# Last chunk's weights requested round by round, a higher filler threshold and a refitted order in a single-core transformer block

## The chip, the core and the metric

The kernel runs on one core of one Trainium2 chip. A core has five instruction queues: TensorE (PE, matrix products), ScalarE (ACT), VectorE (DVE), GpSimd (POOL) and SyncE (SP), which here does nothing but issue transfers. Each executes its queue in order and waits on semaphores that other engines and transfers raise. The metric is the device time of one execution in microseconds (us); lower is better. Before the change the median of three runs is 804.7 us (804.57, 804.7 and 805.7).

## The reference

The program computes one transformer block with adaptive layer norm, on 2048 tokens of width 640, 32 heads of width 20, and a gated MLP of width 1536, all in bfloat16:

```
mod = silu(c) @ w_mod                       # six vectors: sa, ca, ga, sb, cb, gb
h = layernorm(x) * (1 + ca) + sa
q, k, v = split(h @ wqkv)                   # 32 heads of 20
p = softmax(q @ k.T * 20 ** -0.5)           # full attention, 2048 x 2048 per head
x = x + ga * ((p @ v) @ wo)
h = layernorm(x) * (1 + cb) + sb
x = x + gb * (((h @ w_gate) * (h @ w_up)) @ w_down)
```

## The kernel before, in words

**Tiling.** The query tokens are cut into six chunks (`CHUNKS`): two of 512 and four of 256. For every chunk there are eight items, each of four heads; the very last item is split into two halves of 128 queries. An item's scores are made in units of 128 x 512 numbers. Most units go in pairs through ACT, which takes the exponential of a 128x1024 tile (line 1548); the others, in groups of four called quads, get their exponential on DVE by integer arithmetic (lines 1572, 1604, 1612 and 1609, the last also as pieces on POOL, line 1624). Both kinds are then multiplied with V on PE (line 2177). How many quads an item has is fixed by `QUADS`, so the number of ACT exponentials, 812, is fixed too.

**The suffix.** When a chunk's attention is done, its `suffix` follows, in the shadow of the next chunk's attention: the output projection, the second layer norm, the transposed `h2T`, twelve gate-and-up rounds (one per 128 columns of the MLP width, called `fc` 0 to 11), and the down projection. In this text "round k" is the gate-and-up round of the preceding (fifth) chunk for `fc` = k, and "pair k" its two weight tiles, one of `w_gate` and one of `w_up`, 160 KB each. Rounds of the fifth chunk run while the sixth and last chunk's attention runs. PE executes a round as small matmuls on `h2Tt,stg` in line 961, between scores (line 1511) and products with V (line 2177).

**The weight buffers.** Chunks 0 to 4 read gate and up weights through three `stg` buffers for each of the two kinds: pair k+3 may be loaded when round k has been executed. The last chunk's suffix has no attention to hide behind, so most of its weights (`fc` 0 to 9, ten pairs, twenty transfers) get buffers of their own, `stx`, which lie in memory that the attention no longer needs: `fc` 0 to 4 in dead query tiles, the others in the region that the fourth chunk's suffix leaves. Its `fc` 10 and 11 go through `stg`. All are issued by SP in line 1917. SP also issues, for every finished item, four or five small transfers that gather the attention output into `Ocp` (line 1732), a chunk's input `xck` (line 1791) and the output (line 2056).

**What sets the order.** Nothing is scheduled by hand. `build_kernel` makes a list of tasks with durations, dependencies and priorities, and `Sched.run` plays the program through at build time with those durations; the order in which tasks start there becomes each engine's instruction order, and the chip then follows that order, waiting on semaphores. The duration given to a weight load on SP is 400 ns (the default in `dma`), to an `Ocp` transfer 720 ns. Of ready tasks an engine takes the lowest priority number: `Ocp` has 1.05 or 2, chunk four's weights 20 and a bit, the last chunk's 21 and a bit. PE is driven by `pick_pe`: scores first when they can start, then a filler if the modelled activity of the last 3413 ns is under `FILL_HARD`, then projection and MLP rounds if it is under `FILL_MIN`, then products with V, then rounds, then a filler again. A filler (`do_fill`, line 2510) is four matmuls on the identity matrix whose result is not read. `HAM_MIN` is the activity of a 3413-ns window under which the model treats the PE clock as halved; `PE_SWITCH` and `PV_W` are the modelled cost of changing the kind of matmul and of one product with V. `STAGE` overrides the planning parameters while a given item is the oldest unfinished one.

Of the kernel before, what the change touches and what calls it, by code (L numbers as in the profile page):

```python
# [7 lines left out]
ALU = mybir.AluOpType  # L8
AX = mybir.AxisListType
BF16 = mybir.dt.bfloat16  # L10
# [21 lines left out]
STEAL_END = 66197.894  # L32
STEAL_GAP = 200
HAM_W = 3413.3
HAM_MIN = 2550.0
LKTOL = 300.0


# [92 lines left out]
class Sched:  # L131

    def __init__(self):
        self.tasks = []
        self.order = {k: [] for k in ("sp", "act", "pe", "dve", "pool")}
        self.all = []
        self.free_at = {k: T0 for k in self.order}
        self.pend = {k: [] for k in self.order}
        self.readyl = {k: [] for k in self.order}
        self.t = 0.0  # L140
        self.n = 0
        self.progress = 0
# [8 lines left out]
        self.ncold = 0  # L151
        self.nfill = 0
# [197 lines left out]
def emit_program(nc, sched, nsem_dma=56):  # L350
# [123 lines left out]
CHUNKS = ((0, 512), (512, 512), (1024, 256), (1280, 256), (1536, 256), (1792, 256))  # L474
# [6 lines left out]
PV_KEEP = 2  # L481
# [34 lines left out]
D_LATE = 16  # L516
D_RES = 20
PVMIN, PVMAX, PVCAP = 2, 7, 12
# [34 lines left out]
LATEQ_F = 0.35  # L553
QUAD_GAIN = 0.597233983857778
NTERM = 2

STAGE = {
    0: {"D_LATE": 16, "PVMIN": 2, "X_LATE": -179.96, "XDPRIO": 1.343, "LKTOL": 300.0, "FILL_MIN": 4190.746, "HOLD": 95, "TPRIO": 0.75, "PVTOL": 249, "EAGER": 9, "X_HALF": 0.0, "XBACK": 0, "D_RES": 74, "PVCAP": 12, "PVMAX": 14, "STEAL_GAP": 200, "PV_KEEP": 2},
    2: {"DL": 0.376},
    4: {"HOLD": 53.4},  # L560
    5: {"HOLD": 88.7, "STEAL_GAP": 176.5},
    7: {"DL": 0.501},
    9: {"LKTOL": 115.1},
    10: {"X_HALF": 5.8},
    11: {"DL": 0.443, "EAGER": 4, "FILL_MIN": 3731.3, "X_HALF": 38.6},
    12: {"DL": 0.459, "LKTOL": 438.4, "STEAL_GAP": 303.4, "EAGER": 10, "X_HALF": 21.8},
    13: {"DL": 0.417, "FILL_MIN": 4496.3, "STEAL_GAP": 266.2, "X_HALF": 20.9},
    15: {"LKTOL": 166.0, "PVMAX": 5, "EAGER": 10, "XBACK": 1},
    16: {"PVCAP": 10, "PVMAX": 3, "EAGER": 10, "FILL_MIN": 5086.4},
    17: {"X_HALF": -35.2},  # L570
    18: {"EAGER": 3, "X_LATE": -36.1, "HOLD": 42.4, "PVMIN": 1},
    19: {"DL": 0.471, "EAGER": 2, "X_HALF": 94.7},
    20: {"DL": 0.391},
    21: {"EAGER": 6, "FILL_MIN": 4510.3, "X_HALF": 24.2, "D_LATE": 5},
    22: {"PVMAX": 7, "X_HALF": 147.8, "EAGER": 9, "X_LATE": -21.9, "HOLD": 66.8},
    23: {"HOLD": 124.7, "X_HALF": 14.5},
    24: {"DL": 0.464},
    25: {"DL": 0.549, "PV_KEEP": 3, "X_LATE": 36.2},
    26: {"DL": 0.411, "X_LATE": 65.8, "PVMAX": 3, "EAGER": 8},
    27: {"DL": 0.473, "XBACK": 1, "HOLD": 186.0, "FILL_MIN": 3881.8, "X_LATE": -1.8},  # L580
    28: {"X_HALF": 33.6, "FILL_MIN": 4310.0, "XBACK": 0},
    29: {"PVMAX": 7, "X_LATE": -9.2},
    30: {"X_LATE": -109.9, "HOLD": 140.4, "XBACK": 1},
    31: {"X_LATE": 202.7, "D_RES": 21},
    32: {"PVCAP": 11, "X_HALF": -25.7, "X_LATE": 197.5},
    33: {"DL": 0.442},
    34: {"PVMIN": 5, "X_HALF": 27.8, "XBACK": 1},
    35: {"X_HALF": -31.6, "PVMAX": 14},
    36: {"DL": 0.524},
    37: {"X_LATE": -50.4},  # L590
    40: {"XBACK": 1, "HOLD": 36.3},
    41: {"X_LATE": 52.1, "X_HALF": -52.1},
    44: {"X_LATE": -66.5, "EAGER": 4, "D_RES": 10},
    47: {"FILL_MIN": 5302.0},
    48: {"PVCAP": 14, "FILL_MIN": 3192.3},
}
XHALF = 1
STG_G0, STG_G, XC_G = 12, -10, -20
X_LATE = -24.052
X_HALF = 0.0  # L600
# [10 lines left out]
def build_kernel(nc, A_x, A_wqkv, A_wo, B_x, B_w_gate, B_w_up, B_w_down, c, w_mod, out):  # L611
# [7 lines left out]
    NC = len(CHUNKS)  # L619
# [6 lines left out]
    sc = Sched()  # L626
# [87 lines left out]
    DSl = [at("DSS", [128, 4 * 512], I16, d_off + (NB0 + i) * 4096) for i in range(NSS)]  # L714
# [64 lines left out]
    if NALT:  # L779
# [6 lines left out]
        nsq, nsx = nsx, len(stx)  # L786
# [13 lines left out]
    sSS = Slots(list(range(NSS)), "SS")  # L800
# [533 lines left out]
    item_info = {}  # L1334
# [231 lines left out]
    for qi, (it, us) in enumerate(dquads):  # L1566
        st_ = d_state[qi]
        for x, u in enumerate(us):
            cell = {}

            def fp1(e, st_=st_, x=x, cell=cell):
                return e.tensor_scalar(DBl[st_["slot"]][:, x * 512:(x + 1) * 512], bank(cell["b"]), EBIAS, 0.0,  # L1572
                                       op0=ALU.add, op1=ALU.max)
            tp = Task("dve", ps_cost(512), fp1, [], prio=0.8, name=f"P1.{qi}.{x}")
            tp.on_start = lambda task, cell=cell: G.done(cell["b"], task)
            u.task = (tp, cell)
            sc.left += 1
            st_["p1"][x] = tp
    for qi, (it, us) in enumerate(dquads):
        st_ = d_state[qi]  # L1580
        st_["src"], st_["ss"] = {}, {}
# [34 lines left out]
        if X_POOL and qi % X_POOL == X_POOL - 1 and qi < len(dquads) - X_LAST and all(  # L1616
                dquads[z][0] == it for z in range(qi, min(len(dquads), qi + X_TAIL + 1))):
            st_["xby"] = None
            for x in range(X_PIECES):
                w = 2048 // X_PIECES  # L1620

                def fxp(e, x=x, w=w, st_=st_):
                    d = DSl[st_["ss"][0]][:, x * w:x * w + w].bitcast(BF16)
                    return e.tensor_tensor(d, DBl[st_["slot"]][:, x * w:x * w + w].bitcast(BF16), d, ALU.mult)  # L1624
                t = Task("pool", w * POOL_NS + 180.0, fxp, [tm, te], prio=2.0 + .1 * qi + .01 * x, name=f"XP.{qi}")
                t.lk = 2
                t.cond = lambda st_=st_: st_["xby"] != "dve"

                def on_p(task, x=x, st_=st_):
                    if x == 0:  # L1630
                        st_["xby"] = "pool"
                        st_["xd"].dead = True
                        sc.left -= 1
                    xjob[0] = X_PIECES - 1 - x
                    if x == X_PIECES - 1:
                        sB0.done(st_["slot"], task)
                        st_["src"][0] = [task]
                t.on_start = on_p
# [8 lines left out]
            def on_x(task, o0=o0, st_=st_):  # L1647
                o0(task)
                st_["xby"] = "dve"
# [109 lines left out]
    def suffix(ci):  # L1759
# [148 lines left out]
        for fc in range(FT):  # L1908
            use_x = tail and fc < nsx
            wbuf, dm = [], []  # L1910
            for w_, wv in enumerate((wgv, wuv)):
# [4 lines left out]
                def f(e, wv=wv, fc=fc, cell=cell):  # L1916
                    return e.dma_start(cell["t"], wv[:, :, fc * 128:(fc + 1) * 128])
# [115 lines left out]
        for tl in range(ntl):  # L2033
# [5 lines left out]
            for (c_, w) in cuts:  # L2039
# [10 lines left out]
                if tail and TAILX:  # L2050
# [535 lines left out]
```

## Time and profile before

| What | Value |
|---|---|
| Median of the runs | 804.7 us |
| The profiled execution's own time | 806.1 us |
| Span from its first to its last instruction | 804.3 us |
| Mean granted PE clock | 0.998 |
| PE / ACT / DVE / POOL busy in the span | 786.4 / 762.8 / 688.5 / 361.9 us |
| ACT exponentials of line 1548 | 812, 746.8 us busy |
| Filler matmuls of line 2510 | 108, 9.7 us busy |
| Weight loads into `stx` | 20 of 160 KB, issued from 684.1 to 690.9 and from 715.4 to 730.0 us |

Positions in the program are given as microseconds from the start of the span. A row of the timeline has the start, the length, the engine, the line, the operation with its tiles, how many instructions were merged, and in brackets the idle time of the engine just ahead of it with what the profile holds to have ended it. "Busy" counts overlapping instructions once; PE is nearly always busy by this count because matmuls are pipelined and their ends are modelled, so a full PE row does not mean a PE at its peak.

### The profile page before, as it was taken

Reading aid. Unit: us, or ns where it says so; the run is one execution under the profiler, and the core shown is the slowest. Engines: PE = TensorE matmul, PEld = TensorE weight load, DVE = VectorE, ACT = ScalarE, POOL = GpSimd, SP = SyncE. Lnnn points to the kernel's source line nnn. Section 1 sums busy time; section 2 is a strip of 40 time slices with the busy share of each in tenths; the row PEclk is TensorE's granted clock in tenths of the full one; section 3 lists DMA queues with packets and bytes.
Section 4 is the critical chain, followed back from the end, with each engine's and each line's share of the span. In section 5 each row is a group of like instructions: output and inputs, shape, how many; then the busy total and the mean of one; then the engine's idle time right before and its main releaser. Section 6 shows DMA issues by size and latency. Waiting matters only on the chain.

```text
span 804.3 us, 34189 instructions
## 1 busy us (share of the span) xinstructions
PE 786.4 (98%) x14875; PEld 345.9 (43%) x14875; DVE 688.5 (86%) x1355; ACT 762.8 (95%) x847; POOL 361.9 (45%) x373
## 2 busy tenths in 40 slices
PE   8999999999999999999999999999999999998998
PEld 4433423332233232323444444455555554544567
DVE  7989797898999899999877888988898989796654
ACT  6899899999999999999999999999999999998951
POOL 2443436545464643234664433654653434635400
PEclk9999999999999999999999999999999999999999
DMA  9843212202341522101301232100342054527400
GB/s 297 241 122 79 66 53 67 63 24 70 106 107 45 152 66 52 42 7 47 72 18 23 47 78 55 39 16 24 97 88 56 24 121 90 109 58 159 89 22 18
DMA packets 136387, 60.49 MB, mean 75 GB/s; under 512 B 100703, under 2 KB 136239, under 8 KB 136239
## 3 DMA queue, kind: packets, MB, share of 16 engines
q1 hardware_dynamic: 135311, 57.16, 28.0%
q8 instruction: 118, 1.93, 1.0%
q10 hardware_dynamic: 928, 1.15, 0.4%
q14 instruction: 30, 0.25, 0.1%
HBM read 46.70 MB, written 8.99 MB: 69 GB/s over the span
## 4 chain that ended last, share of the span: by engine, by line
PE 60%; ACT 24%; DVE 9%; issue 4%; DMA 2%; SPq 1%; ACTq 0%; DVEq 0%
ACT PP L1548 24%; PE ps_all L1511 20%; PE ps_all L961 18%; PE ps_all L2177 14%; DVE DB L1572 3%; PE ps_all L957 3%; PE ps_all L1221 2%; DMA wm<-in_w_mod_dram 1%; DVE DSS L1612 1%; DVE DSS L1604 1%; DVE DSS L1609 1%; SPq L1732 1%; PE ps_all L2510 1%; PE ps_all L1118 1%; PE ps_all L1157 1%
## 5 line engine op out<-in xcount | busy, mean ns | idle before, releaser
L1548 ACT ACTIVATE PP<-ps_all 128x1024 bf16<-128x1024 f32 x812 | 746.8, 1145 | 7.5 <-PE ps_all L1511 5.2
L1624 POOL TENSOR_TENSOR DSS<-DB,DSS 128x512 bf16<-128x512 bf16 x264 | 300.1, 1157 | 335.3 <-DVE DSS L1612 276.6
L1572 DVE TENSOR_SCALAR DB<-ps_all 128x512 int16<-128x512 f32 x424 | 283.6, 683 | 60.7 <-PE ps_all L1511 58.3
L1511 PE MATMUL ps_all<-QT,KT 32*128 32x256 bf16 (+2 forms) x3136 | 319.1, 307 | 7.0 <-ACT PP L1548 4.1
L1511 PEld LDWEIGHTS ps_all<-QT,KT 32*128 32x128 bf16 x3136 | 89.2, 92 | 229.2 <-ACT PP L1548 191.5
L2177 PE MATMUL ps_all<-PP,Vf 128*32 128x256 bf16 (+2 forms) x2504 | 164.0, 311 | 0.6 <-DVE Vf L1310 0.6
L961 PE MATMUL ps_all<-h2T,stg 128*32 128x256 bf16 (+2 forms) x2272 | 122.3, 303 | 0.8 <-DMA stg<-in_B_w_up_dram 0.5
L2177 PEld LDWEIGHTS ps_all<-PP,Vf 128*32 128x32 bf16 (+1 forms) x2504 | 50.2, 94 | 81.7 <-issue 74.7
L2177 PE MATMUL ps_all<-DSS,Vf 128*32 128x256 bf16 (+1 forms) x1264 | 84.9, 313 | 0.0
L1604 DVE TENSOR_SCALAR DSS<-DB 128x2048 int16<-128x2048 int16 x106 | 73.6, 695 | 0.6
L1612 DVE TENSOR_SCALAR DSS<-DB 128x2048 int16<-128x2048 int16 x106 | 73.1, 690 | 0.0
L961 PEld LDWEIGHTS ps_all<-h2T,stg 128*32 128x32 bf16 x2272 | 51.4, 96 | 30.2 <-issue 20.3
L961 PE MATMUL ps_all<-wd,hprod 128*32 128x320 bf16 (+1 forms) x1384 | 63.2, 279 | 0.0
L1711 POOL TENSOR_TENSOR OTn<-OT,invT 128x256 bf16<-128x256 f32 (+1 forms) x42 | 34.8, 829 | 34.2 <-DVE invT L1709 34.2
L1609 DVE TENSOR_TENSOR DSS<-DB,DSS 128x2048 bf16<-128x2048 bf16 x40 | 49.3, 1231 | 0.0
L2177 PEld LDWEIGHTS ps_all<-DSS,Vf 128*32 128x32 bf16 (+1 forms) x1264 | 31.3, 96 | 20.1 <-issue 8.5
L961 PEld LDWEIGHTS ps_all<-wd,hprod 128*32 128x32 bf16 x1384 | 31.0, 96 | 18.0 <-issue 12.2
L961 PE MATMUL ps_all<-wV,hT 128*32 128x160 bf16 x1280 | 37.6, 234 | 0.6 <-DVE DB L1572 0.2
L1221 PE MATMUL ps_all<-hT,wk 128*32 128x512 bf16 (+1 forms) x360 | 31.6, 382 | 0.4 <-DVE DB L1572 0.2
L1221 PE MATMUL ps_all<-hT,wq 128*32 128x512 bf16 x375 | 31.4, 382 | 0.0
L961 PEld LDWEIGHTS ps_all<-wV,hT 128*32 128x32 bf16 x1280 | 24.0, 96 | 15.4 <-issue 8.4
L961 PE MATMUL ps_all<-wo,Ocp 128*32 128x320 bf16 (+1 forms) x628 | 30.1, 287 | 0.0
(131 smaller groups left out, 525.5 us busy)
## 6 DMA issues: line engine op xcount, KB each, us to landing
stg<-in_B_w_gate_dram SPq DMA_DIRECT2D x62, 160.0 KB
stg<-in_B_w_up_dram SPq DMA_DIRECT2D x62, 160.0 KB
KT<-k_rows SPq DMA_DIRECT2D x112, 32.0 KB
wm<-in_w_mod_dram SPq DMA_DIRECT2D x3, 800.0 KB
x<-in_A_x_dram SPq DMA_DIRECT2D x7, 320.0 KB
k_rows<-KPA SPq DMA_DIRECT2D x16, 128.0 KB
QT<-q_rows SPq DMA_DIRECT2D x32, 64.0 KB
wd<-in_B_w_down_dram SPq DMA_DIRECT2D x1, 1920.0 KB
```

Of the source, the lines that this page charges most:

```text
L957: return lambda e, b: e.matmul(ps[:, b, c0:c0 + n], lhs(), rhs(), start=st, stop=sp)
L961: return lambda e, b: e.matmul(ps[32 * x:32 * x + 32, b, c0 + o:c0 + o + w], lhs()[:, 32 * x:32 * x + 32], rhs() if w == n else rhs()[:, o ...
L1221: f = [lambda e, b_, k=k, x=x: e.matmul(ps[x:x + min(32, w - x), b_, :], wx[:, k, r0 + x:r0 + min(x + 32, w)], hT[tc][:, k, :], tile_posit ...
L1511: ems.append(lambda e, i=i, kt=kt: e.matmul(dstf()[:, i * u.n:(i + 1) * u.n], KT[32 * u.s:32 * u.s + 32, u.j, kt * 128:(kt + 1) * 128], QT ...
L1548: return e.activation(PPs[g % 2][:, cellp["p"], 0:nu * 512], ps[:, b0:b0 + nu, :].rearrange("p b c -> p (b c)"), AFT.Exp, scale=ESCALE)
L1572: return e.tensor_scalar(DBl[st_["slot"]][:, x * 512:(x + 1) * 512], bank(cell["b"]), EBIAS, 0.0, op0=ALU.add, op1=ALU.max)
L1604: return e.tensor_scalar(DSl[st_["ss"][0]][:, :], DBl[st_["slot"]][:, :], 0x7F, 0x3F00, op0=ALU.bitwise_and, op1=ALU.bitwise_or)
L1609: return e.tensor_tensor(d, DBl[st_["slot"]][:, :].bitcast(BF16), d, ALU.mult)
L1612: return e.tensor_scalar(DSl[st_["ss"][1]][:, :], DBl[st_["slot"]][:, :], 0x7F80, 2, op0=ALU.bitwise_and, op1=ALU.bitwise_or)
L1624: return e.tensor_tensor(d, DBl[st_["slot"]][:, x * w:x * w + w].bitcast(BF16), d, ALU.mult)
L1711: f3 = lambda e: e.tensor_tensor(OTn[:, 0:n].rearrange("p (b c r) -> p b r c", c=32, r=2), OT[:, 0:n].rearrange("p (b r c) -> p b r c", c= ...
L2177: ems.append(lambda e, i=i, kt=kt, stt=stt, stp=stp: e.matmul(ps[32 * s:32 * s + mc, bk, 0:u.n], Vf[:, (kt * H + 4 * u.j + s) * VW:(kt * H ...
```

## The change

Three things are changed, and a function is added.

1. The twenty `stx` loads no longer wait for the gathered attention output of the fifth chunk (`oc_ready`). The pair of `fc` waits instead for round `fc // 2` of the fifth chunk: pairs 0 and 1 for round 0, pairs 2 and 3 for round 1, and so on to pairs 8 and 9 for round 4. What frees the memory is waited for as before.
2. Fillers: `FILL_HARD` goes from 3000 to 3500, so a filler goes ahead of other PE work at a higher activity than before, and `HAM_MIN` from 2550 to 3000.
3. The order: `PE_SWITCH` goes from 102 to 105 ns, `PV_W` from 219 to 221 ns, and most entries of `STAGE` are replaced, those of the `DL` kind excepted.

The new function `maybe_sum` would add a quad's two DVE terms on POOL. It returns at once when an item has fewer than `SUM_LEFT` = 100 pieces left; an item has at most 64, so it never acts.

```
-PE_SWITCH = 102.0
+PE_SWITCH = 105.0
-PV_W = 219.0
+PV_W = 221.0
-HAM_MIN = 2550.0
+HAM_MIN = 3000.0
-FILL_HARD = 3000.0
+FILL_HARD = 3500.0
+SUM_LEFT, SUM_Q = 100, 0
 STAGE = {
-    0: {"D_LATE": 16, ..., "D_RES": 74, "PVCAP": 12, "PVMAX": 14, ...},
-    2: {"DL": 0.376},
-    4: {"HOLD": 53.4},
+    0: {"LKTOL": 300.0, ..., "PVCAP": 7, ..., "PVMAX": 14},
+    1: {"FILL_MIN": 2536.8, "XBACK": 2},
+    2: {"DL": 0.376, "FILL_MIN": 5326.4, "D_RES": 24, "PVMIN": 2, "STEAL_GAP": 118.3, "PVCAP": 9},
...
-    40: {"XBACK": 1, "HOLD": 36.3},
-    41: {"X_LATE": 52.1, "X_HALF": -52.1},
-    44: {"X_LATE": -66.5, "EAGER": 4, "D_RES": 10},
-    47: {"FILL_MIN": 5302.0},
-    48: {"PVCAP": 14, "FILL_MIN": 3192.3},
+    39: {"EAGER": 6, "X_LATE": -72.2, "XBACK": 3},
+    42: {"X_LATE": 34.4},
+    43: {"D_RES": 14, "X_HALF": -60.7, "LKTOL": 352.8},
+    45: {"PV_KEEP": 2, "X_HALF": -48.6, "LKTOL": 347.6},
 }
...
+    def maybe_sum(st_, qi, it, tx, te):
+        info = item_info[it]
+        if (qi, 1) not in info["dq"] or info["left"] < SUM_LEFT or sumq[0] + xjob[0] > SUM_Q:
+            return
...
                 t = dma("sp", int(STG_B * 128 * KD * 128 * 2), f,
-                        (sfx_done["qdead"] if fc < nsq else first) + oc_ready[(NC - 2, CHUNKS[-2][1] // 128 - 1)] if use_x else
+                        (sfx_done["qdead"] if fc < nsq else first) + sfx_done["ulist"][fc // 2:fc // 2 + 1] if use_x else
                         kp_use if ci == 0 else [], prio=16 + ci + .01 * fc,
...
         sfx_done["ul"] = u_last[-1:]
+        sfx_done["ulist"] = u_last
...
+                if jj and SUM_LEFT < 99 and st_["src"].get(0) is None:
+                    continue
```

More of the change, by code (lines that the diff above doesn't have):

```diff
@@ L151, in __init__ @@
         self.ncold = 0
+        self.nsum = 0
         self.nfill = 0
@@ L566 @@
[L566 to L574, printed above, removed]
@@ L584 @@
-    31: {"X_LATE": 202.7, "D_RES": 21},
-    32: {"PVCAP": 11, "X_HALF": -25.7, "X_LATE": 197.5},
+    0: {"LKTOL": 300.0, "PVMIN": 2, "X_HALF": 0.0, "D_RES": 74, "D_LATE": 16, "PVTOL": 249, "XBACK": 0, "STEAL_GAP": 200, "PVCAP": 7, "X_LATE": -179.96, "FILL_MIN": 4190.746, "EAGER": 9, "HOLD": 95, "PV_KEEP": 2, "XDPRIO": 1.343, "TPRIO": 0.75, "PVMAX": 14},
+    1: {"FILL_MIN": 2536.8, "XBACK": 2},
+    2: {"DL": 0.376, "FILL_MIN": 5326.4, "D_RES": 24, "PVMIN": 2, "STEAL_GAP": 118.3, "PVCAP": 9},
@@ new lines @@
+    3: {"HOLD": 89.7, "X_HALF": 95.8, "XBACK": 4},
+    6: {"PVMAX": 2, "PV_KEEP": 2, "FILL_MIN": 4261.9, "HOLD": 126.7, "D_LATE": 14},
+    7: {"DL": 0.501, "HOLD": 104.5, "PVMAX": 9, "PVTOL": 291.1},
+    9: {"PVCAP": 11, "X_LATE": -43.4},
+    10: {"STEAL_GAP": 236.0, "X_LATE": 27.2, "D_LATE": 16, "PVCAP": 19, "EAGER": 8, "FILL_MIN": 4539.8},
+    11: {"DL": 0.443, "PVTOL": 349.4, "X_LATE": 38.4},
+    12: {"DL": 0.459, "PVMIN": 1, "EAGER": 9},
+    13: {"DL": 0.417, "HOLD": 117.9},
+    15: {"PVMAX": 8, "EAGER": 8, "X_HALF": -45.4, "X_LATE": 143.1},
@@ new lines @@
+    19: {"DL": 0.471, "HOLD": 55.3, "X_LATE": -24.5},
+    20: {"DL": 0.391, "X_LATE": -10.9},
+    21: {"X_LATE": 161.4, "LKTOL": 262.0},
+    23: {"X_LATE": 127.5, "EAGER": 10, "HOLD": 62.1},
+    24: {"DL": 0.464, "EAGER": 6, "X_HALF": 82.8, "FILL_MIN": 4409.2},
+    25: {"DL": 0.549, "FILL_MIN": 3796.3, "X_LATE": 4.6, "EAGER": 10, "STEAL_GAP": 332.7, "D_RES": 9},
+    26: {"DL": 0.411, "HOLD": 92.2, "EAGER": 8, "PVMIN": 5, "XBACK": 0, "PVTOL": 374.0},
+    27: {"DL": 0.473},
+    29: {"HOLD": 88.3, "XBACK": 1, "PV_KEEP": 2, "X_HALF": 47.9, "EAGER": 6},
@@ L586 @@
+    30: {"FILL_MIN": 5256.4},
+    31: {"LKTOL": 323.3, "HOLD": 121.8, "XBACK": 1},
+    32: {"X_HALF": -47.6, "PVMIN": 7},
     33: {"DL": 0.442},
-    34: {"PVMIN": 5, "X_HALF": 27.8, "XBACK": 1},
-    35: {"X_HALF": -31.6, "PVMAX": 14},
+    35: {"X_LATE": -46.0},
     36: {"DL": 0.524},
-    37: {"X_LATE": -50.4},
-    40: {"XBACK": 1, "HOLD": 36.3},
-    41: {"X_LATE": 52.1, "X_HALF": -52.1},
-    44: {"X_LATE": -66.5, "EAGER": 4, "D_RES": 10},
-    47: {"FILL_MIN": 5302.0},
-    48: {"PVCAP": 14, "FILL_MIN": 3192.3},
+    38: {"X_LATE": 122.3},
@@ L1578, in build_kernel, with fsum, on_s @@
             st_["p1"][x] = tp
+    sumq = [0]
+    def maybe_sum(st_, qi, it, tx, te):
+        info = item_info[it]
+        if (qi, 1) not in info["dq"] or info["left"] < SUM_LEFT or sumq[0] + xjob[0] > SUM_Q:
+            return
+        info["dq"].remove((qi, 1))
+        info["left"] -= 1
+        for u in st_["units"]:
+            left_pv[(it, u.s)] -= len(u.kts)
+        sc.nsum += 1
+        sc.left -= 1
+        sumq[0] += X_PIECES
+        ts = []
+        for x in range(X_PIECES):
+            w = 2048 // X_PIECES
+            def fsum(e, x=x, w=w):
+                d = DSl[st_["ss"][0]][:, x * w:x * w + w].bitcast(BF16)
+                return e.tensor_tensor(d, d, DSl[st_["ss"][1]][:, x * w:x * w + w].bitcast(BF16), ALU.add)
+            t = Task("pool", w * POOL_NS + 180.0, fsum, [tx, te], prio=2.05 + .1 * qi + .01 * x, name=f"SP.{qi}")
+            t.lk = 2
+            def on_s(task, x=x):
+                sumq[0] -= 1
+                if x == X_PIECES - 1:
+                    sSS.done(st_["ss"][1], task)
+            t.on_start = on_s
+            ts.append(sc.add(t))
+        st_["src"][0] = ts
     for qi, (it, us) in enumerate(dquads):
@@ L1627, in build_kernel, with on_p @@
                 t.cond = lambda st_=st_: st_["xby"] != "dve"
-                def on_p(task, x=x, st_=st_):
+                def on_p(task, x=x, st_=st_, qi=qi, it=it, te=te):
                     if x == 0:
@@ L1637, in on_p @@
                         st_["src"][0] = [task]
+                        maybe_sum(st_, qi, it, task, te)
                 t.on_start = on_p
@@ L1645, in build_kernel, with on_x @@
             t.cond = lambda c0=c0, st_=st_: st_["xby"] is None and c0() and xjob[0] >= XBACK
-            def on_x(task, o0=o0, st_=st_):
+            def on_x(task, o0=o0, st_=st_, qi=qi, it=it, te=te):
                 o0(task)
+                maybe_sum(st_, qi, it, task, te)
                 st_["xby"] = "dve"
```

15 lines of the change are left out of this document (removed).

## The prediction

> **What bounds the kernel now.** I read the page first, its head and the rows by slices.
>
> ```profile
> span 804.3 us, 34189 instructions
> PE 786.4 (98%) x14875; PEld 345.9 (43%) x14875; DVE 688.5 (86%) x1355; ACT 762.8 (95%) x847; POOL 361.9 (45%) x373
> ...
> ACT  6899899999999999999999999999999999998951
> ```
>
> ACT is full from the second slice to the third-last, but for two: the fifth (80 to 100 us) and the 37th (724 to 744 us). ACT's exponentials are fixed in number, so they are the metre: the windows of 100 us hold 109 to 111 of them (x column) from 100 to 700 us, 0.91 to 0.92 us each. Here the change can win only where ACT stands idle. ACT's timeline shows where:
>
> ```profile
> 699.60 30.57 ACT L1548 ACTIVATE PP<-ps_all 128x1024 bf16<-128x1024 f32 x33
> 732.25 1.02 ACT L1548 ACTIVATE PP<-ps_all 128x1024 bf16<-128x1024 f32 x1 [2.07 <-PE ps_all L1511]
> 733.72 1.02 ACT L1548 ACTIVATE PP<-ps_all 128x1024 bf16<-128x1024 f32 x1 [0.45 <-PE ps_all L1511]
> 735.26 1.02 ACT L1548 ACTIVATE PP<-ps_all 128x1024 bf16<-128x1024 f32 x1 [0.51 <-PE ps_all L1511]
> 736.48 3.77 ACT L1548 ACTIVATE PP<-ps_all 128x1024 bf16<-128x1024 f32 x4 [0.20 <-PE ps_all L1511]
> ```
>
> The brackets add up to 3.23 us. By starts it is more: the last exponential before the hole began at 729.09 (its 1.09 us end at 730.17), the one at 736.48 is the fourth after it, so 7.39 us passed where four at 0.92 take 3.68: 3.7 us lost. PE's timeline has the cause:
>
> ```profile
> 728.99 0.29 PE L961 MATMUL ps_all<-h2Tt,stg 128*32 128x256 bf16 x4
> 731.42 0.46 PE L961 MATMUL ps_all<-h2Tt,stg 128*32 128x256 bf16 x12 [2.14 <-DVE DSS L1612]
> ```
>
> The windows of 2 us show what it costs (columns: stretch, length, busy of PE, PEld, DVE, ACT and POOL, granted clock, DMA share, GB/s):
>
> ```profile
> 730.00:732.00 2.00, 0.58 (x16) 0.37 (x16) 1.35 (x3) 0.17 (x1) 0.57 (x1) 1.00 0.86 196
> 732.00:734.00 2.00, 2.00 (x42) 1.18 (x42) 0.23 (x1) 1.30 (x2) 2.00 (x3) 0.59 1.14 228
> 734.00:736.00 2.00, 2.00 (x40) 0.91 (x28) 0.79 (x2) 1.49 (x2) 1.93 (x2) 0.56 0.06 14
> ```
>
> PE stands 2.14 us in front of round 4 (with 40 matmuls a round, half-width ones counted as halves, rounds 0 to 3 end at 718.6, 722.2, 726.6 and 729.3). The bracket names DVE, but PE's own semaphore wait there is on two transfers, pair 4, whose landing events are at 730.82 and 731.33. Behind that hole the clock is granted at 0.59 and 0.56 for two rows, which spreads the three later ACT gaps. Of the 3.7 us the wait is 3.16 - 0.92 = 2.2 (ACT starts at 729.09 and 732.25), the low clock the other 1.5. Why pair 4 is late stands in SP's timeline:
>
> ```profile
> 718.64 3.00 SPq L1732 DMA_DIRECT2D Ocp<-OcT  x4
> 721.69 1.38 SPq L1917 DMA_DIRECT2D stg<-in_B_w_gate_dram  x1
> ...
> 725.38 0.53 SPq L1917 DMA_DIRECT2D stx<-in_B_w_gate_dram  x1
> 725.95 0.53 SPq L1917 DMA_DIRECT2D stg<-in_B_w_gate_dram  x1
> 726.53 0.56 SPq L1917 DMA_DIRECT2D stg<-in_B_w_up_dram  x1
> ...
> 731.72 3.80 SPq L1732 DMA_DIRECT2D Ocp<-OcT  x5
> 735.57 0.48 SPq L1917 DMA_DIRECT2D stg<-in_B_w_gate_dram  x1
> ```
>
> Its buffer was free at 722.2, but it was issued at 725.95, behind pair 3 and four of the ten `stx` loads that SP was given at 715; then it took 4.8 us to land with those ahead of it. SP does not rest from 714.98 to 737: it is the short resource here, not the data rate alone.
>
> **The change, part by part.** *The requests.* Removed: ten `stx` loads at 684.1 to 691.5, when nothing waited behind them (the next issue, an `Ocp` at 692.50, was in time), so their leaving gains nothing; and the ten at 715 to 730. Added: four `stx` loads behind each of rounds 0 to 4, twenty in all, in the same 20 us in which SP must issue pairs 3 to 7 and nine `Ocp`. So the same stretch gets ten loads more, but no longer ahead of pairs 3 and 4.
>
> The queue by hand, with durations of this trace: an `Ocp` is 0.76 us (3.00 for four), and pairs go before `stx` by priority. A weight load costs SP from 0.57 us start to start (smooth rows) to 0.77 (13 of them from 721.69 to 731.72, the long issues of 1.38 and 2.03 us included). Three bursts of four, at 642.60, 654.07 and 664.08, took 0.55, 0.62 and 0.74; a batch after a round is such a burst, so I take 0.64. `OcT` is ready at 716.9, so four `Ocp` go to 720.05. Pair 3 and four `stx` end at 723.9; pair 4 is then issued to 725.2 instead of 727.1 and lands, 2.9 us after its second issue as in an empty queue (678.03 to 680.91), at 727.4. Round 4 can start at 729.3: the first hole closes. Its 2.2 and 1.5 us come back: -3.7.
>
> Next in line is pair 6. Five `Ocp` become ready at 728.0 and by priority go ahead of it. Ahead of it stand pairs 3, 4 and 5 (6 loads), ten `stx` and the nine `Ocp`: 720.05 + 16 x 0.64 + 3.85 = 734.1, its second issue at 734.8, landing 737.7. Without the hole, round 6 (started at 739.96 before) is due 3.7 us earlier, at 736.2. So PE waits 1.5 us there. Ends: 0.57 gives 736.6, a wait of 0.4, and none if the new order puts the `Ocp` behind it; 0.77 gives 740.1, 3.9 us. A wait of 1.5 is shorter than the 2.14 that cost the clock, so I count no low clock: +1.6 with the 0.1 by which ACT's loss exceeded PE's. Behind the waiting PE stand scores, so ACT pays all of it. Pair 7 then goes out ahead of the remaining `stx`, whose readers start at 781 us and wait for nothing.
>
> *Fillers.* The page has 108 matmuls of line 2510, 27 fillers; 17 of them lie in 400 to 500 us, where the window holds 109 exponentials against 110 or 111 elsewhere. One exponential, 0.9 us, over 17 fillers is 0.05 each at most. As many again as all 27 would cost 0 (ACT covers them) to 1.4 us (none covered); near the lower end, since the idle rows of ACT there total 0.2 us: +0.3. A gain is excluded where the clock stands at 1.00, which is everywhere but at the hole.
>
> *The order.* Two planned costs move by 1 to 3%, and `STAGE` is mostly new. No instruction is added or removed by this. Its cover is ACT's fullness: from 100 to 729 us the idle rows of ACT sum to under 1 us. What it can move is the spacing, 0.91 to 0.92, against 0.904 for back-to-back exponentials (685 x 0.014 = 9.6 us at stake), and the head, where PE sets the pace and ACT idles 2.1 us in 80 to 100 us. If each 100 us moves by half of the scatter seen between windows (half an exponential), six of them make 2.7 us either way, singly 0.45; as independent moves 1.1. I take 0, bounds -1.5 and +2.
>
> `maybe_sum` and the `HAM_MIN` constant add no instruction: 0.
>
> Sum: -3.7 + 1.6 + 0.3 + 0 = -1.8. The profiled execution took 806.1 us (span 804.3 and 1.8 around it) and lies 1.4 above the median, 0.17%; taken from it the sum gives 804.3, from the median 804.7 it gives 802.9. Less than 0.2%, 1.6 us, I call no change: the runs shown spread by 0.14%.
>
> **The rivals.** *All on time.* SP issues at 0.57 or the order lets pair 6 through: -3.7 + 0.3 = -3.4, 801.3. For it: the smooth rows; against: long issues came in every long stretch.
>
> *The wait moves and takes the clock along* (the other side). With 0.77 us a load round 6 waits 3.9 us, the clock falls again: 3.9 + 0.1 + 1.5 + 0.3 - 3.7 = +2.1, 806.8. It decides from a wait of 2.1, the one known to cost the clock: 2.1 + 0.1 + 1.5 + 0.3 - 3.7 = +0.3; slower by 0.2% it is from 3.4. For it: pair 6 was issued at 735.57 already, with the old order, and landed at 738.98; the old hole hid that. Against: this needs the worst stretch throughout.
>
> The Trainium skill, TensorE: Matmul & The Clock Gate, section "HAM oscillation", warns only of PE gaps over about 3.4 us, a whole idle window. By that rule a wait between 2.1 and 3.4 us would cost no clock, and the change would come to 804.8 at a wait of 3.4 us where the rows give 806.3. The trace speaks against it: 2.14 us were enough.
>
> *The first hole stays*, because another load precedes pair 4 in the new order: about 804.9 with fillers. Against: the tally has 1.9 us to spare at round 4.
>
> *The refitted order costs more than the requests bring*: +2 on top of the forecast, with uncovered fillers +1.1: 806.0. For it: planned durations (400 ns a load) are below every row; against: ACT's fullness.
>
> **How the numbers follow.** Forecast 0.40 (own range 801.7 to 804.1), all on time 0.20, wait with low clock 0.20, hole stays 0.08, order costs 0.12. Faster by over 1.6 us: 0.6 of the first, nearly all of the second, and 0.04 from a lucky order in the others: 0.48. Slower: 0.6 of the third, most of the last, little of the rest: 0.27. The remaining 0.25 is no change. The range runs from 800.6 (all on time with a little from the order) to 806.7 (nearly the clock case in full).
>
> **What would show it.** Right: all `stx` issues after 718, in fours; no PE gap at round 4; a PE gap of about 1.5 us at round 6 with pair 6 issued near 734; clock 1.00 throughout; 109 to 111 exponentials per 100 us. Wrong: a PE gap over 2 us near 736 with granted rows near 0.6; or windows of 100 us with 108 or 112; or a head in which the first hundred us hold more or fewer than 82 exponentials by over two.

## The result: slower by 0.8%, and the profile after

The changed kernel takes 810.9 us (median of 4 runs, 809.3 to 811.6) against 804.6 us before in the same session: a ratio of 1.0076, interval 1.0054 to 1.0098. It is 8.0 us above the forecast of 802.9 and outside its range. The profiled execution took 811.6 us, with a span of 809.8; before it was 806.1 and 804.3. The spans differ by 5.5 us, and that is what has to be found.

Line numbers have moved by a few: exponentials are now line 1544, scores 1507, products with V 2209, the rounds 957, weight loads 1946, `Ocp` transfers 1761, fillers 2542. The head of the page after and two of its rows of 40 slices:

```profile
span 809.8 us, 33954 instructions
PE 789.5 (97%) x14755; PEld 342.5 (42%) x14755; DVE 689.3 (85%) x1352; ACT 764.1 (94%) x848; POOL 370.8 (46%) x381
...
ACT  7899899999999999999999999999999999997951
PEclk9999999999999999999999999999999999999899
```

ACT's low digit still stands in slice 37 (729 to 749 us now), a 7 where it was an 8, and the row of the clock has an 8 in the slice behind it, where it was 9 throughout. The 812 exponentials are the same ones in both kernels, so the start of the n-th can be compared directly, and this gives a running account of what is won and lost (read from the starts of all exponentials in the two traces):

| n-th exponential | start before, us | after, minus before |
|---|---|---|
| 1 | 16.9 | -0.85 |
| 701 | 667.9 | +0.47 |
| 755 | 718.1 | -0.17 |
| 773 | 738.3 | -3.53 |
| 781 | 745.6 | -2.18 |
| 791 | 754.8 | +4.58 |
| 812 | 774.8 | +3.76 |
| end of the span | 804.3 | +5.5 |

Up to the 755th the two stay within 1.5 us of each other. Then the old hole is gone (-3.4), a little is lost at round 6 (+1.4), 6.8 us are lost in the next ten exponentials, 0.8 comes back, and a further 1.7 us is lost behind the attention. ACT's timeline of after shows the same place:

```profile
734.77 5.91 ACT L1544 ACTIVATE PP<-ps_all 128x1024 bf16<-128x1024 f32 x6
741.59 2.85 ACT L1544 ACTIVATE PP<-ps_all 128x1024 bf16<-128x1024 f32 x3 [0.90 <-PE ps_all L1507]
749.27 1.02 ACT L1544 ACTIVATE PP<-ps_all 128x1024 bf16<-128x1024 f32 x1 [4.83 <-PE ps_all L1507]
750.79 1.02 ACT L1544 ACTIVATE PP<-ps_all 128x1024 bf16<-128x1024 f32 x1 [0.50 <-PE ps_all L1507]
752.52 1.02 ACT L1544 ACTIVATE PP<-ps_all 128x1024 bf16<-128x1024 f32 x1 [0.71 <-PE ps_all L1507]
753.94 25.77 ACT L1544 ACTIVATE PP<-ps_all 128x1024 bf16<-128x1024 f32 x28 [0.40 <-PE ps_all L1507]
```

An idle 0.90 at round 6, then 4.83, and three exponentials that come 1.4 to 1.7 us apart instead of 0.92. PE's timeline names the two transfers:

```profile
739.42 0.41 PE L2209 MATMUL ps_all<-PP,Vf 128*32 128x256 bf16 x8
740.71 0.51 PE L957 MATMUL ps_all<-h2Tt,stg 128*32 128x256 bf16 x12 [0.88 <-DMA stg<-in_B_w_up_dram]
...
743.25 0.29 PE L957 MATMUL ps_all<-h2Tt,stg 128*32 128x256 bf16 x4
747.86 0.83 PE L957 MATMUL ps_all<-h2Tt,stg 128*32 128x256 bf16 x12 [4.32 <-DMA stg<-in_B_w_up_dram]
```

By the same count of 40 matmuls a round, round 5 ends at 739.16 and round 6 at 743.54. The first gap is the wait for pair 6: round 6 starts 1.55 us after round 5 has ended, and PE, which has eight products with V in between, stands idle for 0.88 of them. The second, 4.32 us, is the wait for pair 7. The windows of 2 us behind it (columns as in the prediction) show the clock:

```profile
744.00:746.00 2.00, 0.00 (x0) 0.00 (x0) 1.54 (x5) 0.44 (x1) 0.00 (x0) 1.00 0.15 35
746.00:748.00 2.00, 0.14 (x4) 0.14 (x8) 0.00 (x0) 0.00 (x0) 0.00 (x0) 0.71 1.21 261
748.00:750.00 2.00, 2.00 (x32) 0.76 (x24) 0.00 (x0) 0.73 (x1) 0.00 (x0) 0.50 1.33 219
750.00:752.00 2.00, 2.00 (x33) 0.88 (x32) 0.69 (x1) 1.31 (x2) 0.00 (x0) 0.50 1.35 218
752.00:754.00 2.00, 2.00 (x34) 0.77 (x33) 1.44 (x3) 1.08 (x2) 0.07 (x1) 0.58 0.66 108
```

PE is granted half its clock from 746.84 for 6.83 us. During 744 to 746 us the DMA engines are at 0.15: the data path is nearly idle while PE waits for data, so the load had been asked for too late. In the stretch before, in which SP fell behind, the data path was not idle (0.96, the column before the last):

```profile
720.00:738.00 18.00, 17.67 (x434) 9.41 (x429) 15.19 (x30) 17.86 (x21) 8.99 (x9) 1.00 0.96 203
```

SP's timeline says why pair 7 was asked for late:

```profile
735.53 0.52 SPq L1946 DMA_DIRECT2D stg<-in_B_w_gate_dram  x1
736.10 0.53 SPq L1946 DMA_DIRECT2D stg<-in_B_w_up_dram  x1
736.66 0.66 SPq L1946 DMA_DIRECT2D stx<-in_B_w_gate_dram  x1
737.37 1.48 SPq L1946 DMA_DIRECT2D stx<-in_B_w_up_dram  x1
738.89 0.70 SPq L1946 DMA_DIRECT2D stx<-in_B_w_gate_dram  x1
739.64 0.68 SPq L1946 DMA_DIRECT2D stx<-in_B_w_up_dram  x1
740.36 3.59 SPq L1761 DMA_DIRECT2D Ocp<-OcT  x5
743.99 0.83 SPq L1946 DMA_DIRECT2D stg<-in_B_w_gate_dram  x1
744.86 0.52 SPq L1946 DMA_DIRECT2D stg<-in_B_w_up_dram  x1
```

The first pair here is pair 6, the last is pair 7. Pair 7's buffers were free when round 4 ended, at 735.14, but on SP it stands behind pair 6, four `stx` loads and a burst of five `Ocp`, and is issued only at 743.99 and 744.86; it landed at 747.06 and 747.82, and round 7 started at 747.86. SP never rested in between.

The last 1.7 us lies behind the attention. There PE still had this piece to do, the down projection of the fifth chunk, before the last chunk's own rounds:

```profile
784.65 1.95 PE L957 MATMUL ps_all<-wd,hprodt 128*32 128x320 bf16 x52
```

In the stretch from 778 us on there were 48 matmuls of `wd,hprodt` before; now there are 96, and the 28.46 us from the last exponential's end to the end of the span became 30.12. The late rounds are not the reason, although the fifth chunk's last one ends at 767.06 instead of 760.79: the changed kernel with the late half (the last experiment) has no wait, ends its rounds at 758.36, and has the same 96 matmuls behind its last exponential and a tail of 30.36 us. The longer tail belongs to the new order, not to the waits.

### The profile page after: what moved, and what is told of

Same layout as the page of the kernel before. It is cut to its first block, busy times and chain, and to the rows that moved or that the text cites. A ratio compares the mean times of both kernels' runs of the same rounds, so it can differ in the third digit from the quotient of the medians.

```text
span 809.8 us, 33954 instructions
## 1 busy us (share of the span) xinstructions
PE 789.5 (97%) x14755; PEld 342.5 (42%) x14755; DVE 689.3 (85%) x1352; ACT 764.1 (94%) x848; POOL 370.8 (46%) x381
## 4 chain that ended last, share of the span: by engine, by line
PE 61%; ACT 22%; DVE 8%; issue 3%; SPq 3%; DMA 2%; ACTq 0%; DVEq 0%
ACT PP L1544 22%; PE ps_all L1507 21%; PE ps_all L957 17%; PE ps_all L2209 15%; PE ps_all L1217 4%; DVE DB L1568 3%; PE ps_all L953 3%; DVE DSS L1639 1%; SPq L1946 1%; DMA stg<-in_B_w_up_dram 1%; DMA wm<-in_w_mod_dram 1%; PE ps_all L1153 1%; PE ps_all L1904 1%; DVE DSS L1631 1%; SPq L1761 1%
## 5 line engine op out<-in xcount | busy, mean ns | idle before, releaser
L1651 POOL TENSOR_TENSOR DSS<-DB,DSS 128x512 bf16<-128x512 bf16 x272 | 309.2, 1157 | 302.6 <-DVE DSS L1639 236.8
L2209 PEld LDWEIGHTS ps_all<-PP,Vf 128*32 128x32 bf16 x2504 | 50.1, 94 | 80.4 <-issue 74.3
L1639 DVE TENSOR_SCALAR DSS<-DB 128x2048 int16<-128x2048 int16 x106 | 75.9, 716 | 0.1
L1631 DVE TENSOR_SCALAR DSS<-DB 128x2048 int16<-128x2048 int16 x106 | 73.0, 688 | 0.4
L1636 DVE TENSOR_TENSOR DSS<-DB,DSS 128x2048 bf16<-128x2048 bf16 x38 | 47.5, 1251 | 0.0
L1733 DVE STREAM_TRANSPOSE OT<-ps_all 128x256 f32<-128x256 f32 (+2 forms) x49 | 25.7, 524 | 10.1 <-PE ps_all L2209 10.0
```

The costliest lines, as they stand in the source:

```text
L1631: return e.tensor_scalar(DSl[st_["ss"][0]][:, :], DBl[st_["slot"]][:, :], 0x7F, 0x3F00, op0=ALU.bitwise_and, op1=ALU.bitwise_or)
L1636: return e.tensor_tensor(d, DBl[st_["slot"]][:, :].bitcast(BF16), d, ALU.mult)
L1639: return e.tensor_scalar(DSl[st_["ss"][1]][:, :], DBl[st_["slot"]][:, :], 0x7F80, 2, op0=ALU.bitwise_and, op1=ALU.bitwise_or)
L1733: t1 = Task("dve", n * 1.1 + 70, lambda e: e.transpose(OT[:, 0:n], ps[:, item_info[it]["bank"], 0:n].rearrange("p (b q r) -> p b r q", q=3 ...
L2209: ems.append(lambda e, i=i, kt=kt, stt=stt, stp=stp: e.matmul(ps[32 * s:32 * s + mc, bk, 0:u.n], Vf[:, (kt * H + 4 * u.j + s) * VW:(kt * H ...
```

## The experiments

The question was which of the three parts costs the time, and then what makes the requests late: the bytes of the `stx` loads, SP's time, what is ahead in SP's order, or the order itself. All ratios are to the kernel before on the same chip in the same session; its medians were 806.0 for the first four kernels, 805.4 for the next four and 806.3 for the last three.

### One part at a time

**The requests alone.** The kernel before with the new condition only:

```
-   (sfx_done["qdead"] if fc < nsq else first) + oc_ready[...] if use_x else
+   (sfx_done["qdead"] if fc < nsq else first) + sfx_done["ulist"][fc // 2:fc // 2 + 1] if use_x else
...
+   sfx_done["ulist"] = u_last
```

> The kernel before with nothing but the new condition of the stx loads (round fc // 2 instead of oc_ready). Theory A (the requests do it: twenty loads, pairs 3 to 9 and the Ocp transfers in one stretch of SP): no PE gap at round 4, gaps of 1.5 to 5 us at rounds 6 to 8, a low clock after them, and the end 3 to 5 us later than before, 807.6 to 809.6. Theory B (the refitted order does it, the gap of the changed kernel comes from how its order places the loads): with the old planning parameters the gap at round 6 stays under 2 us, 801.5 to 804.6.

Measured: 811.9 us, ratio 1.0080 [1.0055, 1.0106]: the whole loss of the change, and more than the 809.6 that theory A allowed. PE's timeline from 715 to 760 us, only its rows with idle time, in this kernel (line numbers of before):

```profile
730.01 0.46 PE L961 MATMUL ps_all<-h2Tt,stg 128*32 128x256 bf16 x12 [0.98 <-DMA stg<-in_B_w_up_dram]
735.25 0.35 PE L961 MATMUL ps_all<-h2Tt,stg 128*32 128x256 bf16 x8 [1.28 <-DVE hprodt L1951]
739.54 0.29 PE L961 MATMUL ps_all<-h2Tt,stg 128*32 128x256 bf16 x4 [0.93 <-DMA stg<-in_B_w_up_dram]
748.70 0.72 PE L961 MATMUL ps_all<-h2Tt,stg 128*32 128x256 bf16 x12 [2.34 <-DMA stg<-in_B_w_up_dram]
```

With the old order the four gaps are in front of rounds 4, 5, 6 and 8. (The second bracket names DVE, but the last landing event of pair 5 is at 735.16, just ahead of the round.) The one at round 4, 2.14 us before, shrinks to 0.98; in its place three others stand, and the last, 2.34 us, takes the clock (half for 6.83 us from 748.47).

**Everything but the requests.** The changed kernel with the old condition:

```
-   (sfx_done["qdead"] if fc < nsq else first) + sfx_done["ulist"][fc // 2:fc // 2 + 1] if use_x else
+   (sfx_done["qdead"] if fc < nsq else first) + oc_ready[(NC - 2, CHUNKS[-2][1] // 128 - 1)] if use_x else
```

> The changed kernel with the old condition of the stx loads: fillers and refitted order stay. Theory A: the gap at rounds 6 to 8 shrinks to that of before (2.1 us at one round), the time comes within 1.6 us of before, 803 to 806.3. Theory B: 808 to 811, whatever the loads do.

Measured: 806.9 us, 0.6 above the range of theory A, ratio 1.0005 [0.9993, 1.0017]: no change. Fillers and order together are worth nothing here. But its inside is not that of before. ACT's timeline of this kernel:

```profile
699.15 29.70 ACT L1544 ACTIVATE PP<-ps_all 128x1024 bf16<-128x1024 f32 x32
729.25 1.94 ACT L1544 ACTIVATE PP<-ps_all 128x1024 bf16<-128x1024 f32 x2 [0.40 <-PE ps_all L1507]
731.44 41.36 ACT L1544 ACTIVATE PP<-ps_all 128x1024 bf16<-128x1024 f32 x45 [0.25 <-PE ps_all L1507]
```

The old hole is nearly gone with the old requests, by the new order and fillers; the last exponential ends at 772.80, 3.1 us earlier than before. The tail behind it is 32.30 us, 3.8 longer. The new order moves PE's MLP work behind the attention, and pays there what it wins here.

**Fillers alone, order alone.** The kernel before with `FILL_HARD = 3500` and `HAM_MIN = 3000`; and the kernel before with the new `PE_SWITCH`, `PV_W` and `STAGE`:

```
-HAM_MIN = 2550.0        -PE_SWITCH = 102.0
+HAM_MIN = 3000.0        +PE_SWITCH = 105.0
-FILL_HARD = 3000.0      -PV_W = 219.0
+FILL_HARD = 3500.0      +PV_W = 221.0
                         -STAGE = {...}   (the old table)
                         +STAGE = {...}   (the new table)
```

> The kernel before with FILL_HARD 3500 and HAM_MIN 3000 alone. Theory A: fillers under a full ACT cost little, 804.3 to 805.5, with the hole at round 4 as before unless the order there happens to shift. Theory B has no quarrel with that; if fillers were the cause it would be 807 or more, with at least 60 fillers instead of 27.

> The kernel before with PE_SWITCH 105, PV_W 221 and the new STAGE table alone. Theory A: 803 to 806.5, the loads as early as before, so no gap over 2.5 us between 715 and 760 us. Theory B: 807 to 811, with fewer exponentials per 100 us (108 or 109) or gaps of ACT elsewhere.

Measured: 824.9 us, ratio 1.0241 [1.0222, 1.0261], and 822.2 us, ratio 1.0195 [1.0169, 1.0221]. Each alone costs about 2%, far above the ranges of theory A (and the order's also above that of theory B); together nothing. With the new thresholds alone the fillers double, from 27 to 55 groups of four, and ACT is left idle in places where it was full before; from its timeline:

```profile
272.10 67.94 ACT L1548 ACTIVATE PP<-ps_all 128x1024 bf16<-128x1024 f32 x74 [3.27 <-PE ps_all L2177]
...
700.89 53.46 ACT L1548 ACTIVATE PP<-ps_all 128x1024 bf16<-128x1024 f32 x58 [1.73 <-PE ps_all L1511]
757.74 1.02 ACT L1548 ACTIVATE PP<-ps_all 128x1024 bf16<-128x1024 f32 x1 [3.39 <-PE ps_all L1511]
```

By the running account 10.8 us of the loss lie ahead of the last exponential and 8.0 in a longer tail. In the changed kernel, where thresholds and table go together, there are 22 fillers, fewer than before. So the new table holds for the new constants only; the two are one edit. Which of `FILL_HARD` and `HAM_MIN` does the harm is not shown, nor what inside the order alone costs the time: its one profiled execution, at 833.6 us, was the slowest of six.

### What makes the requests late

**Fewer bytes.** The kernel with the requests alone, but each `stx` load brings one of its five slices, a fifth of the data; the last chunk's rounds of `fc` 0 to 9 read that one slice five times, so what the last chunk computes is not the reference.

```
+   if use_x:
+       return e.dma_start(cell["t"][:, 0:1, :], wv[:, 0:1, fc * 128:(fc + 1) * 128])
```

> e1 with each of the twenty stx loads cut to a fifth (32 KB instead of 160; the readers take the one slice that is loaded, so the last chunk's gate and up products are wrong): same number of transfers, same order on every engine. Theory A1 (the data rate is short: about 0.7 us per 160 KB, and SP is held up by a full queue): SP issues at 0.57 us, the gaps of PE at rounds 4 to 9 fall under 1 us in sum, 802 to 805.5. Theory A2 (the number of issues on SP is short, whatever they carry): gaps and time as in e1 within 1.5 us, 808.5 to 812.

Measured: 808.8 us, ratio 1.0032 [1.0010, 1.0054]. PE, ACT, DVE and SP have the same order as with the requests alone; some 3 us of the loss go, but not all. PE's and SP's timelines:

```profile
738.96 0.41 PE L961 MATMUL ps_all<-h2Tt,stg 128*32 128x256 bf16 x4 [3.00 <-DMA stg<-in_B_w_up_dram]
```

```profile
730.06 3.59 SPq L1732 DMA_DIRECT2D Ocp<-OcT  x5
733.69 0.48 SPq L1919 DMA_DIRECT2D stg<-in_B_w_gate_dram  x1
734.22 0.52 SPq L1919 DMA_DIRECT2D stg<-in_B_w_up_dram  x1
```

One gap of 3.00 us is left, in front of round 6, and pair 6 is issued at 733.69, directly behind the five `Ocp`. So it is not the bytes alone. Nor are bytes and SP's time two separate things: the sixteen loads ahead of these `Ocp` take SP 0.65 us each here (719.69 to 730.06) and 0.78 with full loads (719.71 to 732.11), where seven full loads in a row begin to land 0.72 us apart (726.04 to 730.38). Neither theory holds as it was written; whether a full load's issue is slow by itself or because the data path is full is not separated.

**The `Ocp` bursts behind the pairs.** The requests alone, and the last chunk's `Ocp` (but for its last two items) get a priority behind the fifth chunk's pairs:

```
-   prio=1.05 if j >= NSET - 2 else 2
+   prio=1.05 if j >= NSET - 2 else 20.5 if ci == NC - 1 else 2
```

> e1 with the Ocp transfers of the last chunk's items (but the last two) behind the weight pairs of the round and ahead of the stx loads. If the bursts of four or five Ocp (3 to 3.9 us of SP) are what makes pair 6 and the next late, the gaps fall by 2 to 4 us: 805 to 808. If the sum of the transfers is short, the gaps only move to other rounds: 809 to 812.

Measured: 809.6 us, ratio 1.0047 [1.0026, 1.0068]. Perhaps again a part: the interval still overlaps that of the requests alone, and the time lies where the second theory had it. PE's order changes too, from round 6 on, so this is not SP's order by itself. The gaps move, as that theory says: one of 2.69 us stays in front of round 8, at 749.28.

**Both at once.**

> e5 and e8 together: stx loads of a fifth (last chunk's gate and up products wrong) and the last chunk's Ocp behind the weight pairs. e5 kept one hole of 3.0 us at round 6, where pair 6 stood behind five Ocp and ten short loads; e8 alone kept three holes of 4.8 us in sum. Theory A (SP time and data rate add up: each late pair is the sum of what stands ahead of it): with both gone no hole over 0.5 us, clock at 1.00, 801 to 803.5. If another cause makes pairs late here, a hole of 2 us or more stays and the time is 805 or more.

Measured: 805.3 us, ratio 0.9983 [0.9960, 1.0007]: the loss is gone, and the largest gap of PE after 700 us is 0.87 (0.5 was expected at most). All orders are those of the kernel with the `Ocp` behind the pairs, so the step from 1.0047 to 0.9983 is the bytes'. Without that edit of the order the bytes alone did not suffice, nor did the edit without the bytes: neither alone is the cause. What they share is the time until a pair that is needed has passed SP and landed. (The profiled execution, 808.7 us, lost 6.0 us ahead of the 101st exponential, with a low clock at 20 and 95 us, long before the edits act; its span is no measure of them.)

**One pair a round instead of two.** The kernel before, `stx` pair `fc` asked for behind round `fc`:

```
+   ... + sfx_done["ulist"][fc:fc + 1] if use_x else
```

> The kernel before with one stx pair per round (pair fc after round fc) instead of two: the same twenty loads over ten rounds. Theory A (too many loads in too few rounds): 640 KB a round, about 2.6 to 2.8 us of transfer in rounds of 3.5 us, so pairs 3 to 11 come in time but for the Ocp bursts; gaps under 1.5 us in sum and no low clock, 802 to 805.5. If it is the mixing of stx and stg in one queue as such, whatever the rate: 807 to 811.

Measured: 806.3 us, ratio 0.9993 [0.9970, 1.0017]: no change, where theory A had 802 to 805.5 without a low clock. Half the rate of requests is enough to take the loss away, but not to win: a gap of 2.59 us stands in front of round 6, with half the clock for 6.83 us behind it, where 2.14 us stood in front of round 4.

**The plan told 700 ns a load.** The requests alone, and the planner counts 700 instead of 400 ns of SP for a gate or up load of the last two chunks. No instruction is added; only the order can change.

```
+   dur=700.0 if ci >= NC - 2 else 400.0
```

> e1 with the planned SP duration of the weight loads of the last two chunks at 700 ns instead of 400, so that the plan sees SP as slow as the chip has it. Theory C (the holes are the difference between plan and chip; a plan that knows the delay puts other PE work in its place): holes under 1.5 us in sum, the rounds and the down projection later, the tail after the last exponential longer by 1 to 3 us; 805 to 809. If the plan's duration doesn't matter: holes as in e1, 809 to 812.

Measured: 804.4 us, ratio 0.9994 [0.9968, 1.0019]: just under the range of theory C, with a tail of 29.61 us, 1.2 longer than before. ACT's timeline:

```profile
699.62 33.32 ACT L1548 ACTIVATE PP<-ps_all 128x1024 bf16<-128x1024 f32 x36
733.80 16.63 ACT L1548 ACTIVATE PP<-ps_all 128x1024 bf16<-128x1024 f32 x18 [0.86 <-PE ps_all L1511]
751.20 14.83 ACT L1548 ACTIVATE PP<-ps_all 128x1024 bf16<-128x1024 f32 x16 [0.77 <-PE ps_all L1511]
```

Two idle times under 1 us, and the clock stays at 1.00. The same twenty loads, tied to the same rounds, cost 0.8% or nothing, by the number that the planner holds for one of them. SP's timelines show what the number does. Pair 8, the one that cost the clock with the requests alone, is issued there behind sixteen `stx` loads, and here behind eight. Its first load with the requests alone, and in this kernel:

```profile
743.09 0.70 SPq L1917 DMA_DIRECT2D stg<-in_B_w_gate_dram  x1
```

```profile
736.92 1.97 SPq L1917 DMA_DIRECT2D stg<-in_B_w_gate_dram  x1
```

Up to 739.5 us, the start of round 6 with the requests alone, PE's order is the same in both, so the earlier pair is the work of SP's order. From there on PE's order differs as well; how much of the gain is due to each is not separated.

**The late half only.** The kernel before; pairs 0 to 4 as early as before, pairs 5 to 9 behind rounds 6 to 10:

```
+   (sfx_done["qdead"] + oc_ready[...] if fc < nsq else
+    first + sfx_done["ulist"][fc + 1:fc + 2]) if use_x else
```

> The kernel before, its first five stx pairs as early as before, the other five only after rounds 6 to 10; PE's order is the same as before to the instruction. Both theories: pair 4 has no load ahead of it, the hole at round 4 of the kernel before closes with its low clock, 3.7 us less on ACT, and nothing new waits: 800.9 to 802.5. If the time stays at that of before, the hole was hidden by something that ends later, and the metre I used (ACT idle) is wrong.

Measured: 802.0 us, ratio 0.9960 [0.9938, 0.9982]: faster than both kernels. ACT's timeline:

```profile
699.24 62.65 ACT L1548 ACTIVATE PP<-ps_all 128x1024 bf16<-128x1024 f32 x68
762.13 3.77 ACT L1548 ACTIVATE PP<-ps_all 128x1024 bf16<-128x1024 f32 x4 [0.24 <-PE ps_all L1511]
766.09 4.69 ACT L1548 ACTIVATE PP<-ps_all 128x1024 bf16<-128x1024 f32 x5 [0.19 <-PE ps_all L1511]
```

No hole at all, and the clock is 1.00 through the stretch. By the running account the old hole, from the 755th to the 773rd exponential, gives back 3.8 us, and nothing is lost afterwards; the tail is 28.46 us as before. The order of PE, ACT and DVE is that of before, to the instruction, so this is the price of the late pair 4 by itself.

**The changed kernel with the late half.** Its fillers and order, with the condition above:

> The changed kernel with the condition of e7 (first five pairs early, the others after rounds 6 to 10) in place of its own. Theory A: no hole over 1 us, clock 1.00; against the changed kernel 6 to 8 us less; against before it depends on what the order brings by itself: e2 had 0.9 us more than before, with a last exponential 3 us earlier and a tail 3.8 us longer, so 801 to 804.5.

Measured: 804.2 us, ratio 0.9983 [0.9966, 0.9999]. It has no hole either (its last exponential ends at 771.01), but a tail of 30.36 us: the new order's longer tail takes back most of it. Of all kernels here the old order with the late half is the fastest.

## Why the prediction was wrong

**The metre: right. The old hole: right in size, in part by luck.** ACT's exponentials did measure it. The term of -3.7 measured -3.4 in the running account of after and -3.8 with the late half only. But the queue sum behind it was 2.5 to 3 us too early: SP was to be done with pair 4 at 725.2 and was done at 727.73, later than before (727.1), and the pair landed at 730.49, not at 727.4. Round 4 did not wait because round 3 ended only at 731.62 in the new order. In the old order, with the requests alone, 0.98 us of the hole stayed; and with the old requests the new order and fillers gained 2.6 us between the 755th and the 773rd exponential by themselves.

**Pair 6: right in size, by errors that cancel.** The forecast had its second issue at 734.8, landing at 737.7, due at 736.2. The chip had 736.10, 740.62 and 739.16: 1.5 us between due and start, as forecast, of which PE idled 0.88, and +1.4 in the account for +1.6. SP took 0.76 us a load (18 from 721.79 to 735.53), the upper end of the 0.57 to 0.77 that was given, not 0.64; and a load took 4.5 us to land with others ahead of it, not the 2.9 of an empty queue. Twelve `stx` stood ahead of it, not ten. Round 0 itself came 2.5 us later in the new order (718.03 against 715.53), and with it everything that waits for a round. The five `Ocp` did not come ahead of pair 6, which saved 3.6: their `OcT` was ready at 733.62 in the new order, where the forecast took over the 728.0 of before. The forecast called SP "the short resource here, not the data rate alone"; the runs do not separate the two, since with a fifth of the bytes in the `stx` loads SP's issues were faster too, 0.65 us a load against 0.78.

**Pair 7: the step that failed.** "Pair 7 then goes out ahead of the remaining `stx`, whose readers start at 781 us and wait for nothing" has no sum in it; the wait there was put at nothing. The priority decides only while the plan is made; on the chip SP's order stands. A pair's priority goes ahead of `stx`, so the four `stx` ahead of pair 7 must have been given to SP in the plan before pair 7 was ready there (this is argued from the priorities; no run shows the plan's own times); the `Ocp` go ahead of both. From pair 6 to pair 7 the plan allows 6 x 0.40 + 5 x 0.72 = 6.0 us; SP took 8.46, and it had been slipping since pair 3 (18 loads in 13.74 us, where the plan has 7.2). The `Ocp` that did not delay pair 6 delayed pair 7: the forecast named that branch, "none if the new order puts the `Ocp` behind it", as a gain, and didn't ask who stands behind them next. Measured: a wait of 4.3 us and half the clock for 6.83 us, +6.8 us where 0 stood.

**The tail: not in the sum.** The new order leaves 96 instead of 48 matmuls of the down projection behind the attention, with or without waits: +1.7 us where the term for the order had 0.

**Fillers and order.** Together they moved the 755th exponential by -0.2 us, within the bounds given. But the bounds were given for each by itself (0 to 1.4 us, and -1.5 to +2), and by itself each costs some 16 to 19 us, so that their sum came out near zero was luck. ACT's fullness was no cover: with the thresholds alone ACT is not full any more. That it is full because the order was fitted to the constants is likely, not shown. In the kernel without the requests the new order's tail is 3.8 us longer; it was outweighed there by an earlier end of the attention.

**The rivals.** "The wait moves and takes the clock along" is what happened, with 0.20 of the chance and at 806.8 us: one round further on, and with a low clock of twice the length. As a rival to it the Trainium skill was weighed, whose TensorE: Matmul & The Clock Gate, section "HAM oscillation", lets the clock fall behind PE gaps over about 3.4 us. The gap of 4.32 us obeys it. But the runs also have gaps of 2.14, 2.34, 2.59, 2.69, 3.00 and 3.05 us, and behind or within each the grant fell to a half. Of the shorter ones some took the clock (1.94 us, at the start with the fillers alone; 1.80 us, with thin loads and `Ocp` behind) and some did not (1.75 us, fillers alone; 1.60 us, at the start of the kernel before). The measurement decides: here every gap from 2.1 us on took the clock, as the forecast had it. No long gap is needed, though: with thin loads and `Ocp` behind the grant also fell at 20.15 us, in a gap of 0.71 us.

**Of the marks set out,** no gap at round 4, `stx` issues in small batches after 718, and 109 to 111 exponentials per 100 us up to 700 us came true. Pair 6 was issued at 735.5, not near 734, and the gap of PE there was 0.88, not 1.5. A clock of 1.00 throughout did not come true. The mark for being wrong, a gap over 2 us near 736 with granted rows near 0.6, was off by one round: it stood at 743.5.

## What to carry to other kernels

When loads are put into a queue that a plan orders, follow the queue past the first transfer that is late to each of the next ones, and compare the plan's duration of an issue with the one in the trace: here the trace has 0.57 to 0.78 us for a load, and with the requests alone a plan at 0.40 lost 0.8% and one at 0.70 nothing. Optional loads belong where the queue rests, here at 683 to 690 us and again from 744.6 us on, as in the late half; even small batches cost as soon as they stand ahead of something with a deadline. Constants of a planner and the table of overrides that came with them are changed together or not at all.

## What was not expected of the hardware

**The half clock lasts 3.41 or 6.83 us.** Behind the 2.14 us gap of the kernel before, and those of 1.80 and 1.94 us, the grant was a half for 3.41 us; with those of 2.34, 2.59, 2.69, 3.00, 3.05 and 4.32 us it was a half for 6.83 us, twice as long. The forecast had priced every such gap with the 1.5 us of the short one. In the longer case of after three exponentials come 1.4 to 1.7 us apart. What decides between the two lengths is not shown.

**Instruction loading shows among the weight loads.** The page of after, in its part on DMA queues, has this row:

```profile
q8 instruction: 117, 1.92, 1.0%
```

These are 117 packets of 16 KB, one every 7 us on average, each of 0.9 to 1.5 us (in the stretch from 720 to 740 us of after they start at 721.10, 725.99, 732.36 and 737.21). At the last three of them SP's issue of a load takes 1.8, 1.9 and 1.5 us instead of 0.53:

```profile
725.94 1.79 SPq L1946 DMA_DIRECT2D stg<-in_B_w_up_dram  x1
732.26 1.90 SPq L1946 DMA_DIRECT2D stx<-in_B_w_up_dram  x1
737.37 1.48 SPq L1946 DMA_DIRECT2D stx<-in_B_w_up_dram  x1
```

Such long issues stand in the kernel with a fifth of the bytes too (721.82, 726.38 and 736.96 us, of 1.3 to 1.5 us; instruction packets at 721.99, 726.46 and 736.86). In all thirteen traces together 112 issues of a weight load take over 1.2 us, and all but one of them overlap such a packet; but 17 to 32 loads in each trace overlap one and are issued in less. A second sign stands at the landing. Each load has sixteen landing events, and in after the last of them lies 0.7 us behind the fifteenth for pair 6's second load (740.62 against 739.89), and 1.0 us for pair 5's (735.19 against 734.16). That the packets cause either is argued from the coincidence, not shown; no run changed the instruction loading. What follows for a forecast is only that a smooth row of 0.57 us a load is not the rate of a long stretch: with these stops it is 0.76.
